# One 512 KB weight load at the head of a decode kernel, split into two loads by partition parity

## The chip, the cores and the metric

The kernel runs on 1 core of one Trainium2 chip. The metric is device time in microseconds, the median of several executions. The engines are named as in the profile: PE (matmul), DVE (vector), ACT (scalar), POOL (GpSimd) and SP, whose queue issues almost all transfers. The transfers themselves run on the core's 16 DMA engines.

## The reference, cut to what matters

One decode step of a transformer layer for 4 sequences of one token each: layer norm, attention over the last 4096 positions of a K/V cache, output projection with residual, layer norm, a ReLU-gated MLP with residual. All tensors are bf16.

```
B, Sq, D = 4, 1, 576;  Hq, Hkv, Sk, Dh = 32, 16, 16384, 128;  F = 4608
W = min(4096, max(256, Sk // 4))                       # 4096
q = (x @ wq).reshape(B, Sq, Hq, Dh).transpose(0, 2, 1, 3)
k = repeat(k_cache[:, :, Sk - W:, :], 2, axis=1)       # v the same
p = softmax(einsum("bhqd,bhkd->bhqk", q, k) * Dh ** -0.5)
o = einsum("bhqk,bhkd->bhqd", p, v)
h = x + o.transpose(0, 2, 1, 3).reshape(B, Sq, Hq * Dh) @ wo     # the x that gives q is layernorm(x)
g = layernorm(h) @ W_gate
h2 = h + ((g * (g > 0)) * (layernorm(h) @ W_up)) @ W_down
```

Here `wq` is 576 x 4096. Of the input of the layer norm 576 = 512 + 64 features: four chunks of 128 rows of `wq`, and a rest of 64 rows, which is what the change loads in another way.

## The kernel before, in words

The program is written as lists of operations, one list for each engine (`P.op`, `P.dma`). Each operation names the operations that it depends on, and `Prog.emit` turns the names into semaphore waits; every transfer has a semaphore key, and a wait on it is for 16 increments per transfer. The order within an engine is the order in which the lists were written; no scheduler changes it.

**Memory.** `arena` is a large SBUF tensor: 16,384 columns of q weights expanded for the K products, and a ring of `NSLOT` = 4 slots of 16,384 columns (4 MB each). `pp` is a smaller one of `PPW` = 6144 columns; its first 4096 columns are `pT`, later used for the softmax weights, and at the start its first 2048 columns hold the last 64 rows of `wq`.

**The transfers, in the order of SP's queue.** First the last 64 rows of `wq` into `pT` (L251), 512 KB. Then the 512 main rows of `wq` into a ring slot (L255, by `place`), 4 MB. Then sixteen K tiles and sixteen V tiles of 4 MB (L242, in `add_kv`), each into the next ring slot, as soon as the reader of that slot's old content is done: `place` puts the reader (`"QMM"`, `("QK", g)`, `("PV", g)`) into the transfer's dependencies. Then `wo`, the last 64 rows of `W_gate` and of `W_up` (L269 and L271; each to 64 partitions, every other one), the main rows of both (L278), and `W_down` in five pieces (L284). The input x is loaded by ACT's queue.

**The rest of 64 rows.** A matmul contracts over 128 partitions, and the rest has 64 rows. `last_rows` views the rest as 128 half rows, "(r a) n": partition 2r holds the left 2048 columns of row r, partition 2r+1 the right 2048. The features are doubled to match (`xnd_bf`), and `par` is a mask that keeps the even partitions in one copy of the transposed features (chunk 4 of `xnT`) and the odd ones in the other (chunk 5). So the left half of q takes chunk 4 and the right half chunk 5, over the same weights in `pT`.

**The q projection** (`pe_q`, L381 and the helper `mm_same`, L34): chunks 0 to 3 from the ring slot, then chunk 4 from `pT`, eight matmuls of 512 columns for each chunk, into two PSUM banks. The first matmul of chunk 0 waits for the main rows, the first of chunk 4 for the rest. The results are copied (L400, L401), transposed (L386), copied to `q_keep` (L410, L408) and spread by ACT into the arena (L415).

**The main loop** over the 16 tiles: DVE transposes a K tile in place (L424), PE multiplies it with q (L448, L34), softmax per sequence on DVE and ACT, then the products with V (L509, L34) four tiles later. After the loop: output projection (L617), layer norm, gate and up (L666), `W_down` (L690, the last row by L699 and L34), the copy out and the store (L710).

Of the kernel before, what the change touches and what calls it, by code (L numbers as in the profile page):

```python
# [32 lines left out]
def mm_same(e, out, lhsT, rhs, start, stop, tile, pos):  # L33
    return e.add_instruction(mybir.InstMatmult(  # L34
        name=e.bass.get_next_instruction_name(), engine=mybir.EngineType.PE, ins=[e.lower_ap(rhs), e.lower_ap(lhsT)],
        outs=[e.lower_ap(out)], start_tensor_calc=start, stop_tensor_calc=stop, tile_size=tile, tile_position=pos,
        ldweights=False, bass_skip_group_check=True))
# [83 lines left out]
def bass_sequential_preLN__sliding_block_cached__glu_gated_reglu__decode_kernel(  # L121
# [12 lines left out]
    with ExitStack() as es:  # L134
        cnt = [0]

        def sb(name, shape, dt):
            return es.enter_context(nc.sbuf_tensor("sb_" + name, shape, dt))

        P = Prog()  # L140
# [6 lines left out]
        PPW = 6144  # L147
        AW = 2 * QWW + NSLOT * TILE
        arena = sb("arena", [128, AW], BF16)
        pp = sb("pp", [128, PPW], BF16)  # L150
# [25 lines left out]
        xnT = sb("xnT", [128, DC + 1, 32], BF16)  # L176
# [17 lines left out]
        pT = pp[:, 0:4096]  # L194
# [34 lines left out]
        def ring_slot():  # L229
            s = ring[0] % NSLOT  # L230
            ring[0] += 1
            return s
# [15 lines left out]
        def last_rows(W):  # L248
            return W[512:576, :].rearrange("r (a n) -> (r a) n", a=2)

        P.dma("sync", ("L", "wq", 1), lambda e: e.dma_start(out=pT[:, 0:2048], in_=last_rows(A_wq)), "d_wq1")  # L251
        s = ring_slot()
        wq_off = slot0 + s * TILE
        place(("wq", 0), wq_off, TILE, "QMM",
# [8 lines left out]
        for g in range(NTILE - 4, NTILE):  # L263
# [6 lines left out]
            out=bass.AP(tensor=arena, offset=off, ap=[[2 * AW, 64], [1, F]]), in_=B_W_gate[512:576, :]))  # L270
        P.dma("sync", ("L", "gu", 1, 4), lambda e, off=off: e.dma_start(  # L271
            out=bass.AP(tensor=arena, offset=AW + off, ap=[[2 * AW, 64], [1, F]]), in_=B_W_up[512:576, :]), "d_gu_1_4")
# [9 lines left out]
        for r0, r1 in zip(WD_ROWS, WD_ROWS[1:]):  # L282
            place(("wd", r0), wd_off + r0 * D, (r1 - r0) * D, ("DOWN", 1),
                  lambda e, r0=r0, r1=r1: e.dma_start(  # L284
                      out=arena[:, wd_off + r0 * D:wd_off + r1 * D],
                      in_=B_W_down.rearrange("(p r) n -> p (r n)", p=128)[:, r0 * D:r1 * D]))
# [18 lines left out]
                                                in_=c_qm[:, :, :].rearrange("p q (h j) -> p q h j", j=4),  # L305
# [4 lines left out]
                                                in_=to_v[:, :, :].rearrange("p n (k a) -> p n k a", a=4),  # L310
# [14 lines left out]
        for sg in range(2):  # L325
            pool(f"c_toq{sg + 1}", lambda e, sg=sg: e.affine_select(
                out=toq[:, :, :, :], in_=toq[:, :, :, :],
# [40 lines left out]
        def pe_q():  # L368
            for c in range(DC):
                for bk in range(2):  # L370
                    for g in range(4):
                        n = 4 * bk + g
                        w = arena[:, wq_off + c * H * DH + n * 512:][:, 0:512] if c < 4 else pT[:, g * 512:g * 512 + 512]
                        deps = []
                        if bk == g == 0:
                            deps = {0: [("L", "wq", 0), "xnT", "c_xnT"], 4: [("L", "wq", 1)]}.get(c, [])
                        if c < 4 and bk:
                            fn = lambda e, c=c, w=w, g=g, bk=bk: mm_same(e, bank[4 + bk][32 * g:32 * g + 32, :], xnT[:, c, :], w,
                                                                         c == 0, False, (128, 32), (0, 32 * g))
                        else:  # L380
                            fn = lambda e, c=c, w=w, g=g, bk=bk: e.matmul(  # L381
                                bank[4 + bk][32 * g:32 * g + 32, :], lhsT=xnT[:, c + bk if c == 4 else c, :], rhs=w,
                                start=(c == 0), stop=(c == 4), skip_group_check=True)
                        pe("QMM" if bk else "QMM0", fn, deps)
            for blk in range(8):
                pe("QT", lambda e, blk=blk: e.matmul(  # L386
                    bass.AP(tensor=psb, offset=7 * 512 + blk // 4 * 16 + blk % 4, ap=[[4096, 128], [4, 4], [32, 4]]),
                    lhsT=bass.AP(tensor=pp, offset=4096 + blk * 128, ap=[[PPW, 128], [1, 128]]),
                    rhs=bass.AP(tensor=ident_b, offset=0, ap=[[128, 128], [32, 4], [1, 4]]),
                    start=True, stop=True, skip_group_check=True), [f"qev{blk // 4}"] if blk % 4 == 0 else [])  # L390
# [150 lines left out]
        def finish_o():  # L541
            for q in range(4):
                for qd in range(4):
# [6 lines left out]
        pe_x()  # L550
        dve_x()
        pe_q()
        act_q()
        dve_q()
# [6 lines left out]
                                              in_=bass.AP(tensor=e8, offset=0, ap=[[8, 128], [0, 4], [1, 8]])), ["c_e8", "c_selc0"])  # L561
# [47 lines left out]
        for a in range(8):  # L609
            for n in range(2):  # L610
                for j in range(4):
# [4 lines left out]
                    else:  # L616
# [6 lines left out]
                                             in_=bass.AP(tensor=psb, offset=512 + 224, ap=[[4096, 128], [1, 64], [0, 2]])), ["part1"])  # L623
# [27 lines left out]
        for g in range(2):  # L651
            for c in (4, 0, 1, 2, 3):
                part_ = c if c == 4 or (c == 3 and g) else 0
                for m in range(3):
                    for j in range(4):
                        first = m == 0 and j == 0 and (c in (0, 4) or part_ == 3)
                        deps = [("L", "gu", g, part_)] if first else []
# [20 lines left out]
        for i in range(2):  # L678
            dve(("HHT", i), lambda e, i=i: e.transpose(
                out=hhT[:, 576 * i:576 * i + 576].rearrange("p (r q) -> p r q", q=32),  # L680
                in_=bass.AP(tensor=pp, offset=3712 + 18 * i, ap=[[PPW, 128], [1, 18], [36, 32]])), [("HH", m) for m in range(3)])
# [14 lines left out]
        for r in range(36):  # L696
# [3 lines left out]
            for n in range(2):  # L700
                deps = []
# [39 lines left out]
```

## Time and profile before

| what | value |
|---|---|
| median of 3 runs | 377.79 us (377.63 to 377.87) |
| span of the profiled execution | 377.0 us |
| DVE busy | 228.8 us (61%) |
| PE busy | 213.8 us (57%) |
| ACT busy | 53.7 us (14%) |
| bytes read from HBM | 159.58 MB, 423 GB/s over the span |
| the last 64 rows of `wq`: issue to landing | 3.2 us |
| the main rows of `wq`: issue to landing | 12.7 us |
| a K tile, a V tile: issue to landing (median) | 26.3 us, 28.5 us |

The profile is of one execution. Its span is the time from the first to the last instruction on the core; the runs' times include a little more. "Issue to landing" runs from the issuing instruction to the last increment of the transfer's semaphore, so it contains the time that a transfer waits behind earlier ones. "Busy" leaves out waiting; a line number such as L251 is a line of the kernel before.

### The profile page before, as it was taken

What the parts mean: (1) busy time and instruction counts of PE and PEld (TensorE: products, weight loads), DVE (VectorE), ACT (ScalarE), POOL (GpSimd) and SP (SyncE); (2) the same over time, 40 slices, a digit from 0 to 9 for tenths busy, and PEclk for the clock granted to TensorE, in tenths of its full rate; (3) what the DMA queues carried; (4) which work ended last, traced back from release to release, by engine and by line L of the source; (5) the groups of instructions that cost most, each with busy time, mean ns of one, the idle gap of its engine ahead of it and who ended that gap; (6) DMA issues with size and microseconds to landing.
All of it is one profiled execution on the core that took longest, in us unless ns stands there. A gap on an engine that the chain in (4) does not pass through costs nothing.

```text
span 377.0 us, 2556 instructions
## 1 busy us (share of the span) xinstructions
PE 213.8 (57%) x1462; PEld 39.9 (11%) x694; DVE 228.8 (61%) x164; ACT 53.7 (14%) x84; POOL 10.5 (3%) x29
## 2 busy tenths in 40 slices
PE   0404443239919091749282844664655787886658
PEld 0000000001001010001010100110000101002316
DVE  4088878779292969584847778665749433333240
ACT  3093000211000114010101140101010411112010
POOL 8200000000000000000000000000000000000000
PEclk9966666659969788696877786989695968998686
DMA  8999999999999999999999999999999999999996
GB/s 334 445 445 428 405 445 442 396 442 445 398 435 445 442 433 403 442 445 435 407 436 445 435 414 431 441 438 431 417 442 438 426 417 442 418 433 437 427 414 256
DMA packets 6378, 159.74 MB, mean 424 GB/s; under 512 B 728, under 2 KB 864, under 8 KB 1248
## 3 DMA queue, kind: packets, MB, share of 16 engines
q1 hardware_dynamic: 6360, 159.59, 98.7%
q8 instruction: 8, 0.13, 0.1%
q14 instruction: 2, 0.02, 0.0%
q10 hardware_dynamic: 8, 0.00, 0.0%
HBM read 159.58 MB, written 0.00 MB: 423 GB/s over the span
## 4 chain that ended last, share of the span: by engine, by line
DMA 60%; PE 20%; DVE 18%; SPq 1%; issue 0%; ACT 0%
DMA sb_arena<-in_A_k_cache_dram 53%; DVE sb_arena L424 16%; PE psb L34 11%; DMA sb_arena<-in_B_W_down_dram 7%; PE psb L448 4%; PE psb L509 3%; PE psb L690 2%; DVE sb_o_tmp L522 1%; DVE sb_pp L487 1%; SPq L242 0%; PE psb L475 0%; SPq L255 0%; ACT sb_out_sb L709 0%; SPq L251 0%; DVE sb_f L534 0%
## 5 line engine op out<-in xcount | busy, mean ns | idle before, releaser
L424 DVE STREAM_TRANSPOSE sb_arena<-sb_arena 128x8192 f32<-128x8192 f32 (+1 forms) x19 | 139.9, 7366 | 67.3 <-DMA sb_arena<-in_A_k_cache_dram 67.3
L448 PE MATMUL psb<-sb_arena 128*32 128x512 bf16 x256 | 42.8, 633 | 119.6 <-DVE sb_arena L424 119.5
L34 PE MATMUL psb<-sb_arena,sb_pp 128*128 128x512 bf16 (+1 forms) x386 | 108.7, 392 | 0.0
L509 PE MATMUL psb<-sb_arena,sb_pp 128*128 128x512 bf16 x128 | 50.8, 397 | 8.9 <-DVE sb_o_tmp L522 8.9
L519 ACT COPY sb_o_tmp<-psb 32x512 f32<-32x512 f32 x32 | 18.5, 577 | 182.0 <-PE psb L34 181.7
L34 PE MATMUL psb<-sb_arena 128*32 128x512 bf16 x256 | 43.6, 642 | 0.0
L522 DVE TENSOR_TENSOR sb_o_tmp<-psb,sb_fm 32x512 f32<-32x512 f32 x32 | 21.7, 678 | 18.6 <-PE psb L34 18.1
L448 PEld LDWEIGHTS psb<-sb_arena 128*32 128x32 bf16 x256 | 9.5, 119 | 161.9 <-DVE sb_arena L424 132.7
L509 PEld LDWEIGHTS psb<-sb_arena,sb_pp 128*128 128x128 bf16 x128 | 12.8, 100 | 116.6 <-issue 116.6
L526 DVE TENSOR_REDUCE sb_o_sel<-sb_o_tmp 128x128 f32<-128x512 f32 x16 | 17.7, 1106 | 0.5
L467 ACT ACTIVATE sb_pp<-psb,sb_hx 128x1024 bf16<-128x1024 f32 x4 | 4.5, 1113 | 79.4 <-DVE sb_hx L464 79.4
L487 DVE TENSOR_TENSOR sb_pp<-psb,sb_m 128x1024 bf16<-128x1024 f32 x8 | 9.3, 1206 | 4.9 <-PE psb L475 4.9
L482 ACT ACTIVATE sb_pp<-psb,sb_m 128x512 bf16<-128x512 f32 x16 | 9.7, 690 | 14.9 <-PE psb L475 14.9
L525 DVE TENSOR_TENSOR sb_o_tmp<-sb_o_tmp,sb_fm 64x512 f32<-64x512 f32 x16 | 11.0, 689 | 0.5
L415 ACT COPY sb_arena<-sb_q_keep 32x256 bf16<-32x256 bf16 x8 | 9.7, 1451 | 0.1
L690 PE MATMUL psb<-sb_arena,sb_pp 128*32 128x272 bf16 (+1 forms) x70 | 7.6, 396 | 3.7 <-DMA sb_arena<-in_B_W_down_dram 3.7
L401 DVE CAST sb_pp<-psb 128x512 bf16<-128x512 f32 x1 | 2.4, 2427 | 10.5 <-PE psb L381 10.5
L470 DVE STREAM_TRANSPOSE sb_pp<-sb_pp 128x1024 bf16<-128x1024 bf16 x4 | 5.0, 1245 | 5.1 <-ACT sb_pp L467 5.1
L475 PE MATMUL psb<-sb_pp,sb_to_v 128*32 128x256 bf16 x64 | 4.3, 400 | 6.3 <-DVE sb_pp L470 6.3
L690 PEld LDWEIGHTS psb<-sb_arena,sb_pp 128*32 128x32 bf16 x70 | 6.0, 131 | 5.1 <-DMA sb_arena<-in_B_W_down_dram 3.9
L34 PE MATMUL psb<-sb_arena,sb_hnT 128*32 128x384 bf16 x80 | 6.5, 407 | 0.0
L381 PE MATMUL psb<-sb_arena,sb_xnT 128*32 128x512 bf16 x16 | 2.6, 628 | 6.3 <-DMA sb_arena<-in_A_wq_dram 6.3
(120 smaller groups left out, 81.5 us busy)
## 6 DMA issues: line engine op xcount, KB each, us to landing
sb_arena<-in_A_k_cache_dram SPq DMA_DIRECT2D x16, 4096.0 KB, 26.3
sb_arena<-in_A_v_cache_dram SPq DMA_DIRECT2D x16, 4096.0 KB, 28.5
sb_arena<-in_A_wo_dram SPq DMA_DIRECT2D x1, 4608.0 KB, 24.8
sb_arena<-in_B_W_gate_dram SPq DMA_DIRECT2D x1, 4608.0 KB, 27.7
sb_arena<-in_A_wq_dram SPq DMA_DIRECT2D x1, 4096.0 KB, 12.7
sb_arena<-in_B_W_up_dram SPq DMA_DIRECT2D x1, 3456.0 KB, 27.3
sb_arena<-in_B_W_down_dram SPq DMA_DIRECT2D x1, 2160.0 KB, 26.5
sb_arena<-in_B_W_down_dram SPq DMA_DIRECT2D x1, 1440.0 KB, 29.6
```

The lines of the kernel that those rows point to most:

```text
L34: return e.add_instruction(mybir.InstMatmult(name=e.bass.get_next_instruction_name(), engine=mybir.EngineType.PE, ins=[e.lower_ap(rhs), e. ...
L415: act("QW", lambda e, i=i, q=q: e.copy(out=bass.AP(tensor=arena, offset=32 * i * AW + 2 * i + q, ap=[[AW, 32], [512, 16], [136, 4], [32, 4]]),
L424: dve(("TRA", g), lambda e: e.transpose(out=dst, in_=src), [("L", "K", g)] if lo == 0 else [])
L448: fn = lambda e, out_=out_, lhsT=lhsT, rhs=rhs, start=start, stop=stop: e.matmul(out_, lhsT=lhsT, rhs=rhs, start=start, stop=stop, skip_gr ...
L482: act(("EV", b, 0), lambda e, a=a: e.activation(out=bass.AP(tensor=pp, offset=2 * a, ap=[[PPW, 128], [8, 2], [32, 128], [1, 2]]), in_=bank ...
L487: dve(("EV", b, 1), lambda e, n=n: e.tensor_tensor(out=bass.AP(tensor=pp, offset=16 + 8 * n, ap=[[PPW, 128], [32, 128], [2, 4], [1, 2]]), ...
L509: fn = lambda e, lhsT=lhsT, rhs=rhs, k=k, j=j: e.matmul(bank[2 + j], lhsT=lhsT, rhs=rhs, start=(k == 0), stop=(k == 7), skip_group_check=True)
L519: act(("OSC", g), lambda e, j=j: e.copy(out=o_tmp[32 * j:32 * j + 32, 0:512], in_=bank[2 + j][32 * j:32 * j + 32, :]), [("PV", g), ("OSEL" ...
L522: dve(("OSD", g), lambda e, j=j: e.tensor_tensor(out=ot(32 * j, 32), in0=bank[2 + j][32 * j:32 * j + 32, :].rearrange("p (t d) -> p t d", ...
L525: dve(("OS", g), lambda e: e.tensor_tensor(out=ot(64, 64), in0=ot(64, 64), in1=fmb(64, 64), op=ALU.mult), [("OSC", g)])
L526: dve(("OSEL", g), lambda e: e.tensor_reduce(out=o_sel[:, qd, b, :], in_=o_tmp[:, 0:512].rearrange("p (t d) -> p d t", d=DH), axis=AX.X, o ...
L690: return lambda e: e.matmul(out_, lhsT=lhsT, rhs=w[:, lo:hi], start=start, stop=stop, skip_group_check=True)
```

## The change

The load of the last 64 rows is replaced by two loads on the same queue, each of 64 half rows: the left halves (columns 0 to 2047) go to the even partitions, the right halves to the odd ones. The destination is the same 2048 columns of `pp`; `offset=par_ * PPW` starts at partition 0 or 1, and the step `2 * PPW` skips a partition. After both loads `pT` holds what it held before. Each load has a semaphore of its own, and the first matmul of chunk 4 waits for both.

```diff
-        P.dma("sync", ("L", "wq", 1), lambda e: e.dma_start(out=pT[:, 0:2048], in_=last_rows(A_wq)), "d_wq1")
+        for par_ in range(2):
+            P.dma("sync", ("L", "wq", 1 + par_), lambda e, par_=par_: e.dma_start(
+                out=bass.AP(tensor=pp, offset=par_ * PPW, ap=[[2 * PPW, 64], [1, 2048]]),
+                in_=A_wq[512:576, par_ * 2048:par_ * 2048 + 2048]), f"d_wq1{par_}")
...
-                            deps = {0: [("L", "wq", 0), "xnT", "c_xnT"], 4: [("L", "wq", 1)]}.get(c, [])
+                            deps = {0: [("L", "wq", 0), "xnT", "c_xnT"], 4: [("L", "wq", 1), ("L", "wq", 2)]}.get(c, [])
```

Three lines are added ahead of everything else, so line numbers from L252 on are higher by 3 in the changed kernel (the main rows' load is L258, K and V stay at L242, the q matmuls are L384).

## The prediction

> **What bounds the kernel now.** I read four views, from the coarse to the fine: the stretches of the whole span, the SyncE (SP) queue in order of time, the first microseconds in short stretches, and the chain of waits with the last stretches before the end. In the lines of stretches the columns are the stretch, its length, busy time (and count) of PE, weight loads, DVE, ACT and POOL, then the granted TensorE clock, the share of time in which the 16 DMA engines were busy, and GB/s.
>
> ```profile
> 0.00:2.40 2.40, 0.00 (x0) 0.00 (x0) 0.00 (x0) 1.49 (x2) 1.43 (x11) 1.00 0.17 46
> 2.40:372.00 369.60, 210.64 (x1428) 37.60 (x662) 228.33 (x163) 51.84 (x81) 9.07 (x19) 0.79 1.00 430
> 2.40:40.00 37.60, 9.33 (x90) 2.29 (x58) 23.46 (x23) 14.42 (x14) 9.07 (x19) 0.80 1.00 429
> 200.00:240.00 40.00, 21.41 (x140) 3.14 (x63) 30.03 (x20) 6.25 (x11) 0.00 (x0) 0.74 1.00 432
> ```
>
> The reader is to see the 1.00 ahead of the last column: from 2.4 to 372 us the DMA engines never rest, while PE is busy for 211 and DVE for 228 of 370 us. The waits of SP for free slots (231 us in all on PE) are not idle transfer time, since three or four transfers are queued ahead. So the time is a start, 159.6 MB at about 430 GB/s, and a tail; whatever delays the stream at its head delays the end by as much, for there is no idle stretch that could take it up.
>
> ```profile
> 0.80 0.40 SPq L251 DMA_DIRECT2D sb_pp<-in_A_wq_dram  x1
> 1.25 0.41 SPq L255 DMA_DIRECT2D sb_arena<-in_A_wq_dram  x1
> 1.71 35.23 SPq L242 DMA_DIRECT2D sb_arena<-in_A_k_cache_dram  x5
> ```
>
> Columns: start, length, queue, line. The edited transfer (L251) is the very first of the stream, the main rows of the q weights (L255) follow 0.05 us after its issue ends, then the K tiles. So the edit sits at the head, the one place that is exposed.
>
> ```profile
> 1.60:2.00 0.40, 0.00 (x0) 0.00 (x0) 0.00 (x0) 0.40 (x1) 0.31 (x2) 1.00 0.34 113
> 2.00:2.20 0.20, 0.00 (x0) 0.00 (x0) 0.00 (x0) 0.19 (x2) 0.14 (x1) 1.00 0.90 184
> 2.20:2.40 0.20, 0.00 (x0) 0.00 (x0) 0.00 (x0) 0.09 (x1) 0.20 (x2) 1.00 0.49 143
> 2.40:2.60 0.20, 0.00 (x0) 0.00 (x0) 0.19 (x1) 0.00 (x0) 0.20 (x1) 1.00 1.00 392
> 2.60:2.80 0.20, 0.00 (x0) 0.00 (x0) 0.17 (x2) 0.00 (x0) 0.20 (x1) 1.00 1.02 410
> 2.80:3.00 0.20, 0.00 (x0) 0.00 (x0) 0.17 (x2) 0.00 (x0) 0.20 (x1) 1.00 0.96 369
> 3.20:3.40 0.20, 0.00 (x0) 0.00 (x0) 0.20 (x1) 0.00 (x0) 0.20 (x1) 1.00 1.04 430
> ```
>
> Nothing moves until 1.6 us; the first bytes come 0.8 to 1.2 us after the issue at 0.80, and full flow 1.6 us after it. Added up (113 x 0.4 + 184 x 0.2 + ...), 189 KB have started by 2.6, 271 KB by 2.8 and some 513 KB by 3.4 us. There the edited transfer (524 KB) ends, and the main rows go on in the next 0.2 us with no drop: a transfer that is queued early costs no start of its own.
>
> ```profile
> 340.90 26.55 DMA sb_arena<-in_B_W_down_dram
> 367.49 7.54 PE psb L690 x66
> 373.40:373.80 0.40, 0.40 (x9) 0.37 (x9) 0.00 (x0) 0.00 (x0) 0.00 (x0) 1.00 0.47 182
> 373.80:374.20 0.40, 0.40 (x10) 0.37 (x6) 0.00 (x0) 0.00 (x0) 0.00 (x0) 1.00 0.39 138
> ```
>
> The first two lines are of the chain of waits: the end hangs on the landing of the first W_down rows at 367.45 and on the 7.5 us of matmuls behind it, during which the last rows still arrive (until 374.2 us). The DMA share falls to 0.47 and 0.39 there, as some engines have finished their share and others not.
>
> **The change, part by part.** The sum is made against the profiled 377.0 us; the median of the three runs is 377.79, so 0.8 us lie around the span, and I add the difference to that median.
>
> *The issue.* One transfer less and two more on SP: one issue is added, with the main rows, all K and V tiles and the weights behind it in the queue. No row shows a 64-partition issue at the head. The nearest are the L251 issue (0.40 us), and later W_gate's and W_up's last 64 rows, issued to every other partition as here, at 0.49 and 0.60 (L269, L271), beside 0.33 for 128 partitions (L278). With 0.40 and a 0.05 gap the second half is issued at 1.25 and the main rows at 1.70; with 0.60 at 1.45 and 2.10. With the longer delay to first bytes, 1.2 us, the second half is ready at 2.45 (2.65 at worst). The first half's 262 KB are under way until about 2.78, so it comes in time by 0.33 us (0.13). The main rows are ready at 2.90 (3.30), and both halves last until 3.4: in time by 0.5 (0.1). On the path: 0. What hides the issue is the first half's own traffic; without that cover the cost is the added 0.45 to 0.65 us. From below: if an issue of half as many rows takes half of 0.40 us, the first bytes come 0.2 us earlier, so -0.2. From above: the halves pay a start each. From 1.6 to 2.4 us 111 KB moved where 430 GB/s would have moved 344, which is 0.54 us lost; a second start would cost +0.54. I take 0, as the hand-over at 3.4 us is the nearest row.
>
> The Trainium skill, "DMA: Bandwidth & Descriptors", Rules for kernel authors, speaks against the change: two transfers to disjoint partition halves serialize on the same 16 engines, and one 128-partition transfer is to be used. The same page (Anatomy of one DMA) gives a fixed cost of about 2.0 us per DMA, for another issuing path than SP's; if it were paid in full once more the sum would be 379.8, and the row at 3.2 to 3.4 us says that it overlaps.
>
> *The bytes.* The same 512 KB in the same rows of 4 KB to the same partitions, but each half now skips every other 4 KB of the source and every other partition. Every other partition was also written by the 64-row loads that start at 335 us; the stretches 335 to 341 moved 341, 493 and 493 GB/s, a mean of 442, so that costs nothing. A skipping source is found in the W_down chunks (a slice of each row): 429 GB/s from 360 to 368 us, 415 from 368 to 372, where the slices get short. At 415 instead of 430, 524 KB take 0.04 us more; I take that. Bounds: 0 and 0.04.
>
> *The wait.* PE's first matmul of chunk 4 waits for two semaphores instead of one. Behind it are the remaining q matmuls and then the transposes of q and ACT's copies (L415). The data landed at 4.0 us and the matmul runs at 17.35, so the wait is met 13 us ahead. The q path as a whole ends with ACT at 31.61 us (21.88 + 9.73), and the first QK matmul starts at 32.51 after DVE's transpose: 0.9 us of cover for one more satisfied wait. On the path: 0; uncovered it is one PE instruction, below the 0.11 us of a weight load.
>
> Sum: 0 + 0.04 + 0 = +0.04 us, so 377.0 in the profile and 377.83 in the median (377.79 + 0.04). The unknowns put the likeliest case between 377.6 (-0.2) and 378.4 (+0.54 +0.04).
>
> **The rivals.**
>
> *Each transfer pays its own start* (slower). The place is the head of SP's queue: if the second half and then the main rows began to flow only when the one before was through, 0.54 us would be lost twice, 1.08 in all: 377.79 + 1.08 + 0.04 = 378.9. For it: the halves hold 0.6 us of traffic each, and an issue takes 0.45 to 0.65, so the reserve is thin, 0.13 us at worst. Against: the unbroken hand-over at 3.4 us. It decides once both starts show; one alone stays at 378.4. The rule of the Trainium skill named above ("DMA: Bandwidth & Descriptors", Rules for kernel authors) points to this rival.
>
> *The sixteen DMA engines run in another stagger* (either side). At the end they finish one after the other: the shares 0.63, 0.62, 0.47 and 0.39 of the four stretches of 0.4 us from 372.6 to 374.2 add up to 0.84 us of work for all engines spread over 1.6 us. Evened out, the stream would end 0.76 us earlier. The first stretch, too, ran at 429 GB/s where later ones had 432, which is 0.26 us in 37.6. If the smaller first transfers set the engines off better spaced, both are gained: 377.79 - 0.76 - 0.26 = 376.8, faster. If they set them off worse, the same amounts are lost: 378.8. For it: the head is where the spacing begins, and the last engine decides the end. Against: the three runs lie within 0.24 us, so small differences of the start do not grow, and each engine gets the same count of rows in both halves.
>
> **How the numbers follow.** Forecast 0.53; starts paid twice 0.16; stagger better 0.16; stagger worse 0.15. A difference of 0.2%, 0.76 us, is about what a measurement of this kernel can tell from no change, so same means 377.03 to 378.55. Faster is the better stagger, 0.16; slower the two others, 0.31; same 0.53. The range from 377.0 to 379.0 holds the forecast and both slower cases but for their tails (0.08 left out above), and the upper part of the faster one (0.10 left out below); the likeliest case alone is 377.6 to 378.4.
>
> **What would show it.** In the changed profile SP has two issues of 0.33 to 0.60 us ahead of the main rows, and the DMA share stays at about 1.0 in every 0.2 us from 2.4 to 3.6 us. If it drops to half there for 0.2 us or more, the starts are paid. The transpose of the first K tile starts at 23.74 us plus the delay of the head; the same delay must be found again at the first W_down landing (367.45) and at the end. If the transpose is at 23.7 and the landing has moved by over 0.5 us, the stagger or the rate in between did it, and the stretches of 40 us say where. PE's chunk 4 still follows chunk 3 without a pause at 17.35. The prediction is wrong if the median is outside 377.03 to 378.55.

## The result, and the profile after

The changed kernel takes 380.69 us in the median (380.16 to 380.80), the kernel before 377.69 (377.63 to 377.87): a ratio of 1.0076 (95% interval 1.0064 to 1.0088), 3.0 us slower. The span of the profiled execution went from 377.0 to 378.9 us, so that the two profiles show 1.9 of the 3.0 us. Where a run has both figures on record, its time lies 1.2 to 1.3 us above its span. By this estimate the profile of the kernel before is of an execution of about 378.2 us, 0.5 above its median; that of the changed kernel is of its fastest run, 380.16 us, 0.5 below its median. Times are medians of the runs; of the runs below one is left out, of `e17_late_main_k0_later`, which took 436.45 us where the other four took 378.97 to 380.36.

The issues on SP's queue at the head of the changed kernel (start, length, line):

```profile
0.80 1.18 SPq L252 DMA_DIRECT2D sb_pp<-in_A_wq_dram  x2
2.02 0.59 SPq L258 DMA_DIRECT2D sb_arena<-in_A_wq_dram  x1
2.66 36.57 SPq L242 DMA_DIRECT2D sb_arena<-in_A_k_cache_dram  x5
```

The two halves take 0.55 and 0.58 us to issue (1.18 is both with the gap), where the whole transfer took 0.40; with the gaps, the main rows go out at 2.02 instead of 1.25 us, 0.77 later.

The first microseconds of the changed kernel, with two longer stretches (the last two columns are the DMA share and GB/s):

```profile
1.60:2.00 0.40, 0.00 (x0) 0.00 (x0) 0.00 (x0) 0.40 (x1) 0.31 (x2) 1.00 0.09 12
2.40:2.60 0.20, 0.00 (x0) 0.00 (x0) 0.19 (x1) 0.00 (x0) 0.20 (x1) 1.00 0.88 328
2.60:2.80 0.20, 0.00 (x0) 0.00 (x0) 0.17 (x2) 0.00 (x0) 0.20 (x1) 1.00 0.87 348
2.80:3.00 0.20, 0.00 (x0) 0.00 (x0) 0.17 (x3) 0.00 (x0) 0.20 (x1) 1.00 1.10 348
3.00:3.20 0.20, 0.00 (x0) 0.00 (x0) 0.20 (x2) 0.00 (x0) 0.20 (x1) 1.00 0.74 266
3.20:3.40 0.20, 0.00 (x0) 0.00 (x0) 0.20 (x2) 0.00 (x0) 0.20 (x1) 1.00 0.96 369
2.40:40.00 37.60, 9.33 (x90) 2.15 (x58) 21.26 (x23) 14.43 (x14) 9.07 (x19) 0.82 1.00 424
200.00:240.00 40.00, 21.25 (x138) 2.88 (x62) 29.29 (x19) 6.25 (x11) 0.00 (x0) 0.79 1.00 433
```

Of the kernel before, the one row of these stretches that was not shown yet:

```profile
3.00:3.20 0.20, 0.00 (x0) 0.00 (x0) 0.12 (x2) 0.00 (x0) 0.20 (x1) 1.00 1.07 410
```

The stream starts later, and from 2.4 to 3.4 us it stays below the rate of before: the five rows have 332 GB/s in the mean, against 402 before, and a share of 0.91 against 1.02. (Later, with 32 KB packets counted where they start, such short stretches say nothing.) In the middle of the run the rate is the same as before, 433 against 432 GB/s. So the loss is of the head.

When the first K tile has landed is seen from the first transpose on DVE, of the kernel before and of the changed kernel (start, length, and what ended the idle time):

```profile
23.74 8.71 DVE L424 STREAM_TRANSPOSE sb_arena<-sb_arena 128x8192 f32<-128x8192 f32 x1 [1.10 <-DMA sb_arena<-in_A_k_cache_dram]
```

```profile
26.04 8.71 DVE L427 STREAM_TRANSPOSE sb_arena<-sb_arena 128x8192 f32<-128x8192 f32 x1 [1.01 <-DMA sb_arena<-in_A_k_cache_dram]
```

It is 2.30 us late at 24 us, and the end is 1.9 us late: all of it was lost in the first microseconds, and none later. But the bytes are not 2.3 us late. The trace also has the time of each increment of a transfer's semaphore: 16 of them for each transfer, the last of which is the landing. Sorted, their first, ninth and last are (us):

```
                      before                     changed
main rows      13.54   13.69   13.92      14.27   14.81   16.31
first K tile   23.38   23.47   23.72      23.98   24.53   26.01
last W_down   372.89  374.27  374.72     373.21  374.64  376.68
```

The Trainium skill, "DMA: Bandwidth & Descriptors", Why a DMA increments its semaphore by 16 and not by 1, says that each engine that takes part in a transfer posts one increment when its own share has landed. The 16 separate times in this trace agree with that; so the columns are the fastest, a middle and the slowest engine. At the first K tile the fastest is 0.6 us late, the middle one 1.1, the slowest 2.3. What has grown is the distance from the middle to the slowest, from 0.25 to 1.48 us; at the end it is 2.0 us, against 0.45 before. The span follows the slowest: 377.0 - 374.72 and 378.9 - 376.68 are both 2.2 to 2.3 us.

The second half is uneven already: its increments come at 3.90 (first), 4.16 (ninth) and 5.11 us (last), where those of the whole transfer came at 3.81, 3.89 and 4.04.

At the end of the changed kernel PE shows it too (waits of PE's matmuls):

```profile
369.46 5.19 PE L693 MATMUL psb<-sb_arena,sb_pp 128*32 128x272 bf16 x50 [3.71 <-DMA sb_arena<-in_B_W_down_dram]
375.29 1.66 PE L693 MATMUL psb<-sb_arena,sb_pp 128*32 128x272 bf16 x20 [0.64 <-DMA sb_arena<-in_B_W_down_dram]
```

Before, the 66 matmuls ran through once they had begun at 367.49. Now they begin at 369.46 and stop once more for a later piece of `W_down`. In the stretch from 374 to 376 us:

```profile
374.00:376.00 2.00, 1.36 (x22) 0.96 (x18) 0.00 (x0) 0.00 (x0) 0.00 (x0) 1.00 0.23 89
```

(of the changed kernel; the next line is of the kernel before)

```profile
374.00:376.00 2.00, 1.18 (x17) 0.71 (x12) 0.43 (x1) 0.40 (x1) 0.00 (x0) 1.00 0.03 11
```

the DMA engines are still busy for 0.23 of the time (0.03 before): a few engines work while the others are done.

### The profile page after: what moved, and what is told of

It is laid out like the page before. It is cut to its first block, busy times and chain, and to the rows that moved or that the text cites. A ratio compares the mean times of both kernels' runs of the same rounds, so it can differ in the third digit from the quotient of the medians.

```text
span 378.9 us, 2558 instructions
## 1 busy us (share of the span) xinstructions
PE 211.9 (56%) x1462; PEld 39.6 (10%) x694; DVE 228.8 (60%) x164; ACT 53.7 (14%) x84; POOL 10.5 (3%) x29
## 4 chain that ended last, share of the span: by engine, by line
DMA 57%; PE 21%; DVE 20%; SPq 1%; issue 1%; ACT 0%
DMA sb_arena<-in_A_k_cache_dram 48%; DVE sb_arena L427 16%; PE psb L34 13%; DMA sb_arena<-in_B_W_down_dram 9%; PE psb L451 4%; PE psb L512 3%; DVE sb_o_tmp L525 1%; DVE sb_pp L490 1%; PE psb L478 1%; PE psb L693 0%; DVE sb_pp L473 0%; DVE sb_hx L456 0%; ACT sb_pp L470 0%; SPq L252 0%; SPq L287 0%
## 5 line engine op out<-in xcount | busy, mean ns | idle before, releaser
L451 PE MATMUL psb<-sb_arena 128*32 128x512 bf16 x256 | 43.0, 631 | 118.7 <-DVE sb_arena L427 118.7
L34 PE MATMUL psb<-sb_arena,sb_pp 128*128 128x512 bf16 (+1 forms) x386 | 106.4, 385 | 0.0
L512 PE MATMUL psb<-sb_arena,sb_pp 128*128 128x512 bf16 x128 | 49.9, 390 | 8.9 <-DVE sb_o_tmp L525 8.9
L34 PE MATMUL psb<-sb_arena 128*32 128x512 bf16 x256 | 44.4, 646 | 0.0
L693 PE MATMUL psb<-sb_arena,sb_pp 128*32 128x272 bf16 (+1 forms) x70 | 6.8, 356 | 4.4 <-DMA sb_arena<-in_B_W_down_dram 4.3
L384 PE MATMUL psb<-sb_arena,sb_xnT 128*32 128x512 bf16 x16 | 2.5, 628 | 8.7 <-DMA sb_arena<-in_A_wq_dram 8.7
L678 DVE TENSOR_TENSOR sb_pp<-psb,sb_pp 128x384 bf16<-128x384 f32 x3 | 1.5, 551 | 9.0 <-PE psb L669 9.0
L669 PE MATMUL psb<-sb_arena,sb_hnT 128*32 128x384 bf16 x40 | 4.2, 406 | 3.9 <-DVE sb_hnT L650 2.0
```

What stands on the lines that cost most here:

```text
L34: return e.add_instruction(mybir.InstMatmult(name=e.bass.get_next_instruction_name(), engine=mybir.EngineType.PE, ins=[e.lower_ap(rhs), e. ...
L451: fn = lambda e, out_=out_, lhsT=lhsT, rhs=rhs, start=start, stop=stop: e.matmul(out_, lhsT=lhsT, rhs=rhs, start=start, stop=stop, skip_gr ...
L512: fn = lambda e, lhsT=lhsT, rhs=rhs, k=k, j=j: e.matmul(bank[2 + j], lhsT=lhsT, rhs=rhs, start=(k == 0), stop=(k == 7), skip_group_check=True)
```

## The experiments

Three theories. *Place*: two small transfers ahead of the main rows delay the issue of these, the 16 DMA engines pick them up late and unevenly, and the most delayed engine sets the end. *Shape*: the skipping source or destination, or 64 partitions instead of 128, is slow by itself. *K issue* (added later): the issue of the K tiles disturbs the pick-up. In the expectations N, L and E stand for parts of *place* (two issues ahead, the late issue, the most delayed engine), S and H for *shape*, and K for *K issue*. Here are the results together; the K tile's three columns are the first, ninth and last increment, "issued" is when SP issues the main rows, and the ratio is to the kernel before in the same comparison, estimated from the runs, so that it is not exactly the quotient of the medians given below. Increments and span are of one execution of each kernel.

```
kernel                      issued   first K tile          span    ratio (95%)
before                       1.25   23.38 23.47 23.72     377.0
changed                      2.02   23.98 24.53 26.01     378.9   1.0076 (1.0064-1.0088)
e1_dense_halves              2.04   24.55 24.72 25.02     377.9   1.0028 (1.0016-1.0039)
e5_dense_source              2.03   23.92 24.35 24.70     377.5   1.0038 (1.0022-1.0054)
e6_dense_dest                2.04   24.49 25.65 25.93     378.7   1.0049 (1.0032-1.0065)
e4_second_on_act             1.40   23.78 23.93 24.19     376.9   1.0010 (1.0000-1.0019)
e12_main_between             1.41   23.80 24.25 24.62     377.4   1.0022 (1.0012-1.0033)
e11_two_wide                 1.72   24.15 24.75 26.27     379.1   1.0054 (1.0040-1.0068)
e13_late_1p6                 1.59   23.54 23.72 25.46     377.2   1.0052 (1.0034-1.0070)
e15_late_1p8                 1.80   23.87 24.08 26.24     379.1   1.0053 (1.0036-1.0071)
e9_late_main                 1.94   24.37 25.70 26.09     379.0   1.0060 (1.0045-1.0075)
e14_late_2p4                 2.40   24.05 24.33 24.62     377.5   1.0020 (1.0010-1.0030)
e3_main_first_one            0.80   23.44 23.71 24.22     377.0   1.0006 (0.9997-1.0015)
e2_main_first_two            0.79   23.61 23.86 24.09     376.9   1.0007 (0.9997-1.0016)
e17_late_main_k0_later       1.94   24.02 24.98 25.47     378.4   1.0042 (1.0028-1.0057)
e18_halves_k0_later          2.03   23.93 24.38 24.57     377.4   1.0051 (1.0032-1.0070)
e19_k0_later                 1.25   23.29 23.50 23.73     376.5   0.9997 (0.9988-1.0007)
e7_two_engines               1.23   23.25 23.38 23.56     383.5   1.0180 (1.0164-1.0195)
```

**Is it the skipping?** Two transfers of 64 partitions, each dense on both sides:

```diff
-                out=bass.AP(tensor=pp, offset=par_ * PPW, ap=[[2 * PPW, 64], [1, 2048]]),
-                in_=A_wq[512:576, par_ * 2048:par_ * 2048 + 2048]), f"d_wq1{par_}")
+                out=pT[64 * par_:64 * par_ + 64, 0:2048],
+                in_=last_rows(A_wq)[64 * par_:64 * par_ + 64, :]), f"d_wq1{par_}")
```

> Two transfers as in the changed kernel, but split into partitions 0 to 63 and 64 to 127, so that each reads 256 KB in one piece and writes neighbouring partitions. Theory N (two small issues ahead of the main rows are what costs: SP issues the main rows at 2.02 instead of 1.25 us and the 16 DMA engines set off unevenly): stays near the changed kernel, 379.7 to 381, the slowest DMA engine ends the main rows 1 us or more behind the middle one. Theory S (the skipping form costs: 0.55 to 0.58 us an issue against 0.40, and engines that start late): back to 377.5 to 378.3, issues near 0.40 us.

Dense on the source only (the `in_` line above, with the stepped `out`):

> The changed kernel with each of its two transfers reading 256 KB in one piece, still to every other partition. The last 64 rows of the q weights come to other partitions, so q is another one; all work is kept. Theory S with the skipping source as the cause: 377.5 to 378.3. Theory S with the skipping destination as the cause, or theory N: 379.7 to 381.

Dense on the destination only (the `out` line above, with the skipping `in_`):

> The changed kernel with its skipping source, but each transfer to 64 neighbouring partitions. The last 64 rows of the q weights come to other partitions, so q is another one; all work is kept. Theory S with the skipping destination as the cause: 377.5 to 378.3. Theory S with the skipping source, or theory N: 379.7 to 381.

Medians: 379.14, 379.43 and 379.99 us against 378.15 of the kernel before; the first two lie between the ranges of the theories, the third in that of theory N. The two dense halves cost 1.0 us already, without any skipping, so *shape* in the sense of skipping is not the whole; nor is it nothing, as the changed kernel is clearly above the dense split (1.0076 against 1.0028). The intervals of the two mixed forms overlap with that of the dense split, so the skip cannot be put down to one side. The issues on SP do not depend on it; of the dense split:

```profile
0.80 1.19 SPq L252 DMA_DIRECT2D sb_pp<-in_A_wq_dram  x2
2.04 0.59 SPq L258 DMA_DIRECT2D sb_arena<-in_A_wq_dram  x1
```

The same two issues in 1.19 us, and the main rows at 2.04. In the profiled execution of the dense split all engines are late alike (24.55 to 25.02, a width of 0.5 us); in that of the changed kernel the width is 2.0 us.

**Is it the 64 partitions?** Two transfers to all 128 partitions, each with half of the columns:

```diff
+                out=pT[:, 1024 * par_:1024 * par_ + 1024],
+                in_=last_rows(A_wq)[:, 1024 * par_:1024 * par_ + 1024]), f"d_wq1{par_}")
```

> Two transfers at the head as in the changed kernel, but each to all 128 partitions with half of the columns (rows of 2 KB). If 64 partitions are what makes issue and start slow (0.55 to 0.58 us, first packet 2.13 us): issues of about 0.40 us, first packet at 1.83 us, 377.7 to 378.5. If it is the second transfer as such: like the split into two dense halves, 378.8 to 379.5.

380.28 us against 377.9, though it issues fast:

```profile
0.80 0.87 SPq L252 DMA_DIRECT2D sb_pp<-in_A_wq_dram  x2
1.72 0.42 SPq L258 DMA_DIRECT2D sb_arena<-in_A_wq_dram  x1
```

So 64 partitions do cost 0.15 us an issue (0.55 to 0.58 against 0.41), and a first packet at 2.13 instead of 1.87 us, but without them the loss is nearly as large, 2.4 us. (This split has packets of 2 KB instead of 4 KB, which could add to its loss; the kernel with the late issue alone, below, has not.) It needs no skipping and no 64 partitions.

**Is it the late issue of the main rows?** The second half on ACT's queue, so that SP can go on:

```diff
-            P.dma("sync", ("L", "wq", 1 + par_), lambda e, par_=par_: e.dma_start(
+            P.dma("scalar" if par_ else "sync", ("L", "wq", 1 + par_), lambda e, par_=par_: e.dma_start(
```

> The changed kernel with its second transfer issued by ACT's queue, ahead of the load of x, so that SP issues the main rows right after the first half. If the late issue of the main rows is what costs: main rows issued at about 1.40 us, 377.5 to 378.5. If the two transfers cost by themselves, wherever they are issued: 379.7 to 381.

SP's queue:

```profile
0.80 0.56 SPq L252 DMA_DIRECT2D sb_pp<-in_A_wq_dram  x1
1.40 0.58 SPq L258 DMA_DIRECT2D sb_arena<-in_A_wq_dram  x1
```

378.52 against 378.15, at the upper edge of the first range: the same two skipping halves, with the main rows at 1.40 us, cost 0.1%. Then the converse, the kernel before with nothing but a wait ahead of the main rows:

```diff
         place(("wq", 0), wq_off, TILE, "QMM",
               lambda e: e.dma_start(out=arena[:, wq_off:wq_off + TILE], in_=main_rows(A_wq)), key=f"slot{s}")
+        P.q["sync"][-1].deps.append("c_m40")
```

> The kernel before, whose issue of the main rows waits for a POOL instruction that ends at 1.91 us, so that they are issued at about 2.0 us instead of 1.25, as late as in the changed kernel; the edited transfer stays whole. Theory L (the late issue of the main rows alone is what lets the DMA engines run dry): main rows fully landed 1 us or more later than 13.92, time 378.9 to 380.5. Theory H (the two half transfers themselves start late and unevenly, and the main rows were in time at 2.0): landed by 14.3, time within 0.4 us of before.

380.28 against 377.9. SP's queue and the first transpose:

```profile
0.80 0.40 SPq L251 DMA_DIRECT2D sb_pp<-in_A_wq_dram  x1
1.94 0.33 SPq L255 DMA_DIRECT2D sb_arena<-in_A_wq_dram  x1
...
26.11 8.71 DVE L425 STREAM_TRANSPOSE sb_arena<-sb_arena 128x8192 f32<-128x8192 f32 x1 [1.08 <-DMA sb_arena<-in_A_k_cache_dram]
```

The edited transfer is whole, is issued in 0.40 us and starts at 1.83 us as before; only the next issue is 0.69 us late, and the first transpose is at 26.11 against 26.04 in the changed kernel. The late issue alone is enough for 2.4 us, of the change's 3.0; the intervals of the two overlap.

**How late is too late?** The same with waits for other POOL instructions (`c_idb`, `c_xnT`, `c_m41`):

> The kernel before, whose issue of the main rows waits for a POOL instruction that ends at 1.56 us: issued at about 1.6 us instead of 1.25. By the forecast's own reckoning (data ready 1.2 us after the issue, edited transfer under way until 3.4) nothing is lost: 377.6 to 378.3. Theory L (the reserve is far thinner, because some engines need 2 to 3 us from issue to their first packet, and a first large packet that was not queued ahead takes 1.4 to 2 us instead of 1.21): a loss between that of 1.25 and of 1.94 us, 378.5 to 380.3.

> The kernel before with the main rows issued at about 1.8 us, by a wait for a POOL instruction that ends at 1.77 us. If the loss is one of unevenness, worst where the main rows come while the engines run dry one by one: 379.5 to 380.5, most delayed engine 1 us or more behind the middle one. If e9 with 1.94 us was a chance: below 379.3.

> The same with a POOL instruction that ends at 2.38 us: main rows issued at about 2.4 us. Theory L with a loss that grows with the lateness: 0.47 us more than with the issue at 1.94, 380.5 to 381.3. If the loss is a fixed one, paid once when the engines run dry: 380.0 to 380.5.

The issue of the main rows in e13, e15 and e14:

```profile
1.59 0.33 SPq L255 DMA_DIRECT2D sb_arena<-in_A_wq_dram  x1
1.80 0.33 SPq L255 DMA_DIRECT2D sb_arena<-in_A_wq_dram  x1
2.40 0.33 SPq L255 DMA_DIRECT2D sb_arena<-in_A_wq_dram  x1
```

379.56, 380.43 and 378.76 us against 378.1; the first two lie in the ranges of the late issue. Already the issue at 1.59, 0.34 us late, costs 0.5%; one at 2.40 costs least of the four, 0.2%. So neither of the two ideas about e14 holds (a loss that grows, or a fixed one). What separates the four in their profiled executions is the width, in the table: at 1.59 one engine is 1.1 us behind the next (the fifteenth increment of the first K tile is at 24.32, the last at 25.46); at 1.80 and 1.94 several are 1 to 2 us apart; at 2.40 all of them are late by 0.7 to 0.9 us, but within 0.6 us of each other. The single packets say the same: the first packets of the main rows start between 3.44 and 3.68 us in the kernel before, 3.63 and 5.58 in the changed one, 3.14 and 5.55 in e9, where nine of the 16 start after 5.0; in e14 all start from 3.60 to 4.82, 13 of them by 4.27. From the issue that is 1.2 us for the first engine of e9 and e14, 1.6 for that of the changed kernel, and up to 3.6 for the last. These first packets are slower as well, 1.4 to 2.0 us for most in the changed kernel, where 1.21 is usual for 32 KB.

The runs of a kernel in this regime scatter: e13 from 378.47 to 380.36, e5 from 378.54 to 380.64, where the kernel before has 377.6 to 378.7 in all comparisons. So a span in the table, which is of one execution, does not always match its ratio (e13, e18). That the engines are set apart differently from one execution to the next would explain it, but is not shown, as each kernel has one trace.

**Does the place decide?** The main rows first, then the rest whole, and then as the change's two halves:

```diff
-        P.dma("sync", ("L", "wq", 1), lambda e: e.dma_start(out=pT[:, 0:2048], in_=last_rows(A_wq)), "d_wq1")
         s = ring_slot()
...
               lambda e: e.dma_start(out=arena[:, wq_off:wq_off + TILE], in_=main_rows(A_wq)), key=f"slot{s}")
+        P.dma("sync", ("L", "wq", 1), lambda e: e.dma_start(out=pT[:, 0:2048], in_=last_rows(A_wq)), "d_wq1")
```

> The kernel before with the main rows issued first and the last 64 rows (one transfer) second; they are needed 3 us after the main rows land. If a head is good when large packets are queued first, since then nothing can run dry: 377.0 to 377.8, at or below before, the 16 engines ending the main rows within 0.5 us of each other. If the small packets at the head are what sets the engines off evenly: 378.2 to 379.

> The changed kernel with its two half transfers issued behind the main rows instead of ahead of them. If the loss is of the place (nothing long is queued behind small transfers): near the kernel that issues the main rows first and the rest whole, 377.9 to 378.6. If skipping rows and partitions costs by itself: 379 or more.

378.23 and 378.17, against 377.9 and 378.1: no difference to the kernel before that can be told, in either; e3 lies at the lower edge of the second expectation, so the small packets at the head are worth little in themselves, 0.3 us by the medians and 0.6 by the upper end of the interval. In e2:

```profile
1.24 1.16 SPq L256 DMA_DIRECT2D sb_pp<-in_A_wq_dram  x2
2.45 0.65 SPq L242 DMA_DIRECT2D sb_arena<-in_A_k_cache_dram  x1
```

The very transfers of the change, with 1.16 us of issue instead of 1.18, are free behind 4 MB, which keep the engines busy for some 10 us. And with the main rows between the two halves, all on SP:

> The changed kernel with the main rows issued between the two halves, at about 1.40 us, all on SP. Theory L: as with the second half on ACT's queue, 378.2 to 378.9. If a first transfer of 64 partitions spoils the start by itself: 379.5 or more.

378.90 against 378.1, 0.2%, at the upper end of the first range: a later start of the first packet (2.14 instead of 1.83 us) and a small width are left.

**Does the most delayed engine set the end?** The kernel before with six small transfers behind the third K tile (a product with the fifth K tile also waits for them; it loses nothing by it, as that tile is transposed only from 60.66 us on and the last of them landed at 51.19):

```diff
+            if g == 2:
+                for i in range(6):
+                    P.dma("sync", ("L", "z"), lambda e, i=i: e.dma_start(
+                        out=arena[2 * i:2 * i + 2, QWW:2 * QWW],
+                        in_=A_wq[0:4, :].rearrange("(p r) n -> p (r n)", r=2)), "d_z")
...
+                            if g == 4:
+                                deps.append(("L", "z"))
```

> The kernel before with six more transfers of 2 rows of 16 KB (nothing uses them), queued behind the third K tile where the queue is full, which should go to two of the 16 DMA engines: 96 KB more for each, 3.6 us at the 27 GB/s of one engine. Theory E (the most delayed engine sets the end and no later transfer evens it out): 2.5 to 4 us slower, 380.3 to 381.7, and the spread of landings stays to the end. Rival (the bytes are shared out again or only the sum counts): 0.2 MB at 430 GB/s, 0.5 us slower.

384.77 against 377.9: 6.9 us slower for 0.2 MB in 160. The twelve 16 KB packets lie between 42 and 50 us, two at a time, and took 0.61 to 1.99 us each, more than the 0.6 reckoned; as two chains they add up to 6.7 and 7.4 us. The last landing of `W_down` is at 381.29, 6.6 us later than before, and the fifteenth increment at 379.91, with the ninth at 376.36. The end of e7:

```profile
374.00:376.00 2.00, 1.93 (x19) 1.73 (x21) 0.00 (x0) 0.00 (x0) 0.00 (x0) 0.56 0.70 279
376.00:378.00 2.00, 2.00 (x22) 1.60 (x20) 0.00 (x0) 0.00 (x0) 0.00 (x0) 0.59 0.12 52
378.00:380.00 2.00, 1.24 (x19) 0.85 (x16) 0.00 (x0) 0.00 (x0) 0.00 (x0) 1.00 0.11 43
```

For the last 4 us the share is 0.11 to 0.12, two engines of sixteen. Work that is laid on two engines at 45 us is still theirs alone at 380: nothing shares it out again. The price of the theory was too small, its mechanism holds, and the rival's 0.5 us is out.

**Is it the issue of the K tiles?** Theory K, tried on e9, on the changed kernel and on the kernel before:

```diff
             add_kv("K", g)
+            if g == 0:
+                P.q["sync"][-1].deps.append("mv")
```

> The kernel e9 (main rows issued at about 1.94 us), with the first K tile issued only after a DVE instruction that ends at about 4.2 us; the main rows keep the engines busy until 14 us, so that by itself costs nothing. Theory K (the issue of the K tiles disturbs the engines' start on the main rows): loss below 1 us, 378 to 378.9, main rows landed by 15.2. Theory L without it (the pick-up of transfers by nearly empty engines is uneven by itself): as e9, 379.7 to 380.6.

> The changed kernel with the first K tile issued only after about 4.2 us. Theory K: 378.3 to 379.4. Theory L without it: as the changed kernel, 380 to 381.

> The kernel before with the first K tile issued only after about 4.2 us: control. Both theories: within 0.4 us of before; under theory K a little below it is possible, 377.4 to 378, as the first main rows (1.25 us mean there against 1.21 later) would be undisturbed.

379.90, 379.71 and 378.06, against 378.12. The K tiles are issued from 4.1 to 4.5 us on, and the first two are still 0.4 and 0.5% slower; e17 is within what its rival foretold, e18 below it and above theory K, with an interval that overlaps the changed kernel's. Theory K falls as the cause; a share of it is not excluded. The control is unchanged.

None of the kernels tried is clearly faster than the kernel before; e19 and the two with the main rows first are equal to it.

## Why the prediction was wrong

*What bounds the kernel* was right: the transfer stream, with its head exposed. The rate in the middle is unchanged (433 against 432 GB/s), and 2.3 us lost by 24 us are found again at the end as 1.9.

*The issue.* Its length was at the upper end of the bounds, 0.55 and 0.58 us, so the main rows went out at 2.02 us (1.70 taken, 2.10 at worst). The step that failed is the next one, the overlap that hides the later issue: "The main rows are ready at 2.90 (3.30), and both halves last until 3.4: in time by 0.5 (0.1). On the path: 0." It took the 1.2 us from the issue to the first bytes of the first transfer for all transfers and all engines. In the changed kernel the first packet of the main rows starts at 3.63 on the first engine and at 5.58 on the last, 1.6 and 3.6 us after the issue; and the second half, taken as through by 3.4, ends at 3.60 on the first engine and at 4.77 on the last. The hand-over at 3.4 us in the kernel before was taken as proof that nothing is paid; it showed a transfer that had been issued over 2 us ahead, with no word on how much of that was needed. e13 shows that 0.34 us less is already too little for one engine: 15 start the main rows by 3.91 us, the last at 4.50.

*The median from the span.* The 0.8 us between the profile of before and the median mixed two executions: within one, the distance is 1.2 to 1.3 us. That changed nothing in the forecast, which adds its difference to the median.

*From below and above.* The gain of 0.2 us by a shorter issue did not come: the first packet starts at 2.13, not 1.83 us. The bound of 0.54 us from above was for a start lost by all engines alike, and missed what one engine can lose.

*The bytes.* Right as far as it went: behind the main rows the two skipping halves cost nothing (e2). Ahead of them they leave the engines more uneven than dense halves; why is open.

*The wait.* Right: chunk 4 follows chunk 0 by 3.39 us as before (19.75 - 16.36, against 17.35 - 13.97).

*The rivals.* The stagger of the sixteen engines, at 0.15 on its bad side, is what happened; its size was taken from the widths seen in the kernel before (0.76 + 0.26 us), where the change made a new one: from the middle to the slowest engine 1.48 us at the first K tile and 2.0 at the end, beside 1.1 us for the middle engine. "The three runs lie within 0.24 us, so small differences of the start do not grow" was true and beside the point: they do not grow, but neither do they shrink (e7). The rival of two starts named the place and the point from which it decides, and expected every engine to pay alike; that is nearer to e14 and e1. The rule of the Trainium skill ("DMA: Bandwidth & Descriptors", Rules for kernel authors: not two transfers to disjoint partition halves) had the sign right: the dense halves cost 1.0 us here. Two skipping halves behind a long transfer cost nothing that can be told (e2), a case that the rule does not distinguish.

*Open.* Why one or several engines pick up the next transfer more than 1 us later than their neighbours, while an issue at 2.40 sets them off nearly together; why the skipping halves cost 3.0 us and the dense ones 1.0 with the same issue times; and how much the width changes from one execution to the next.

## What to carry to other kernels

At the head of a stream that is bound by transfers, issue a long transfer first, or second at the latest, and put small ones behind it: a later issue of the long one by 0.3 to 0.8 us cost 1.0 to 3.0 us here, and one by 1.15 us (e14) 0.7. Do not read the slack of an issue from a hand-over without a gap; try it by delaying the issue. Look at the 16 increments of a landing and not only at the last one: a width among the engines stays to the end, and the slowest sets the time.

## What the runs showed of the hardware

- As the first of SP's queue, a transfer to 64 partitions takes 0.55 to 0.57 us to issue, one to 128 partitions 0.38 to 0.41, whatever is skipped; the first packet comes at 2.13 to 2.30 us instead of 1.81 to 1.87. (The main rows, to 128 partitions, also take 0.57 to 0.59 when they are issued behind such a half.)
- A later issue can cost less than an earlier one: main rows at 1.94 us, 2.4 us lost; at 2.40 us, 0.7 us.
- 96 KB more on each of two DMA engines, in a stream of 160 MB, cost 6.9 us.
- The first 32 KB packets of the main rows took 1.4 to 2.0 us on 15 of the 16 engines in the changed kernel, against 1.21 in the stream.
